# Two attention and gMLP layers on one core: the later weights' scales found by a DMA read-back in two batches, and the weights' splits moved within the first layer

## The chip, the core and the metric

The kernel runs on one core of a Trainium2 chip. The metric is the device time of one execution, in microseconds (us), as the median of several runs. "Layer" below means one attention block followed by one gMLP block; the program runs two layers with the same weights.

## What is computed

With `phi(t) = t + 1` for positive t and `exp(t)` otherwise, and x of 2048 rows by 640 columns:

```
x = A_x
x = x + A(layernorm(x));  x = x + B(layernorm(x))
x = x + A(layernorm(x));  x = x + B(layernorm(x))

A(x):  q, k, v = x @ wq, x @ wk, x @ wv            # 32 heads of 20
       for 4 segments of 512 rows:
           o = (1 - g) * softmax(q k^T * scale + mask) v + g * (phi(q) M) / (phi(q) z)
           M, z += phi(k)^T v, sum phi(k)
       return o @ wo                                # wo 640 x 640
B(x):  z = gelu(x @ w_in)                           # w_in 640 x 1728
       z1, z2 = z[:, :864], layernorm(z[:, 864:])
       return (z1 * (w_sp @ z2 + b_sp)) @ w_out     # w_out 864 x 640
```

Products run in fp16 with each operand held as a high and a low half. A weight is first scaled by a power of two that comes from its largest absolute value, then split: `h = fp16(w * s)` on ScalarE, `l = fp16(w * s - h)` on VectorE (`split_scaled`, L80). So before a weight can be split, its largest element over all 128 partitions must be known on every partition.

## The kernel before

Each layer has three phases: `phase1a` (attention, class `Attention`), `phase1b` (the last rows' output projection, layernorm, both halves of w_in) and `phase2` or, in the second layer, `phase2s` (the w_sp product and w_out).

**The attention** is a software pipeline in steps. `Attention.run` (L1376) walks t from below 0 to past 192. In each step PE multiplies one chunk of a pair of heads: `mp` (scores for the row maxima, read by VectorE's `mx` reduction at L1304) and `es` (scores for the exponentials, read by ScalarE's `P` at L1297). Then come the fp16 halves of P (`PH` on ScalarE at L1314, `PL` on GpSimd at L1315), and the product with v (`pv`, L1341). One `P` activation belongs to one step, so 192 of them make one attention. Tiles `mp`, `es` and `pv` have one buffer each: PE's next chunk waits for the readers of the last one.

Around the pipeline several generators are run, each yielding the step at which it wants to go on: `fills` (next rows' layernorm), `background` (the weights), `dense` (the q, k, v and output projections in between) and `reads`. PE's order is as written; the other engines' instructions are ordered at build time by a list scheduler, which works with priorities (`tc.high_priority`, and `issue_after` for what must not go earlier). Each engine's queue, and SP's queue that issues nearly all DMAs, is then run in order: an instruction that waits holds up all behind it.

**The weights, in the first layer only.** `head` (L950) scales and splits wq, wk and wv before step 0. In `background` (L1459), `other_scales` (L179) loads all of wo, w_in and w_out in 32 tiles from step -8 on, 0.75 step apart, and reduces each on VectorE (`wap<-wmst`, L192) in a pool of two buffers that other tiles use as well. At steps 50 to 53 the maximum is carried over the partitions by TensorE: a transpose (`wtp`), a reduction, a scaled identity (`wdg`), and a product with ones (`wbc`). From step 55 on wo is loaded again and split in five tiles, and from step 69 the half of w_in called i1 in ten (`Weight.load`, L106). The other half, i0, is split by `phase1b` in five tiles of 864 columns after the attention. `keep` (L130) writes the halves to DRAM; the second layer reads them back instead.

**The end of the attention.** `phase1b` first brings the first two tiles of rows to the transposed form `th` (`load`, `attn_out`, `xn_t`): a load of x1, layernorm (`lnst`, `lnmv`, `lnve` on VectorE, `lnrs` on GpSimd, `xn` on VectorE), its halves `xnhl` (ScalarE, VectorE) and a DMA transpose. `first` is a context that lets these begin in the last steps of the attention. Then PE multiplies, for each tile of 128 rows, 30 matmuls with i1 and 30 with i0 (`zp`, L316).

Of the kernel before, what the change touches and what calls it, by code (L numbers as in the profile page):

```python
# [9 lines left out]
F32 = mybir.dt.float32  # L10
# [36 lines left out]
WNAMES = ["v", "q", "k", "o", "i0", "i1", "u"]  # L47
# [18 lines left out]
def pow2_spread(g, psum, tag, dg, c0, n):  # L66
# [3 lines left out]
    nc.tensor.matmul(bc[:, :n], g.ones8[:n, :], dg[:n, :n], start=True, stop=True)  # L70
    pw = g.pw[:, c0:c0 + n]
    nc.vector.tensor_copy(pw, bc[:, :n])
# [15 lines left out]
class Weight:  # L88
# [17 lines left out]
    def load(self, stage, width=864, tag="wst", keep=True):  # L106
# [4 lines left out]
        if self.made:  # L111
# [30 lines left out]
def attn_weights(g, ctx, wv, wq, wk, wo, w_in, w_out):  # L142
# [6 lines left out]
    g.wi = [Weight(g, "i0", 4, w_in, 0, FH), Weight(g, "i1", 5, w_in, FH, FH)]  # L149
# [4 lines left out]
    g.esc, g.rq, g.rk, g.gq, g.gk, g.sig, g.epsd, g.yw, g.zi, g.pofs = s(0), s(1), s(2), s(3), s(4), s(5), s(6), s(7), (s(8), s(9)), s(10)  # L154
# [24 lines left out]
def other_scales(g, a, pool, psum, tag):  # L179

    nc = g.nc
    last = None
    for i, w in enumerate((g.wo, *g.wi, g.wu)):
        width = D if w.cols == D else w.cols // 2
        j = 0
        for k in range(w.nk):
            n = min(128, w.dram.shape[0] - 128 * k)
            for c in range(0, w.cols, width):
                t = a.bg.tile([128, D], F32, tag="bg", name="wmst")[:n, :width]
                nc.sync.dma_start(t, w.dram[k * 128:k * 128 + n, w.c0 + c:w.c0 + c + width])  # L190
                if last is not None:
                    nc.vector.tensor_reduce(*last, AX.X, ALU.max, apply_absolute_value=True)  # L192
                last = g.wap[:n, i, j:j + 1], t
                yield True
                j += 1
    nc.vector.tensor_reduce(*last, AX.X, ALU.max, apply_absolute_value=True)
    yield 50
    nc.vector.tensor_reduce(g.wam[:, 3:7], g.wap, AX.X, ALU.max)
# [4 lines left out]
    nc.vector.tensor_scalar(g.yw, g.pw[:, 0:1], g.pw[:, 3:4], 2.0 ** -19, ALU.mult, ALU.mult)  # L203
    nc.vector.tensor_scalar(g.sc[:, 8:10], g.pw[:, 4:6], 2.0 ** -24, None, ALU.mult)
# [1400 lines left out]
```

## Time and profile before

| | us |
|---|---|
| median of 3 runs | 2323.73 (2322.91 to 2328.16) |
| the profiled execution | 2331.88 |
| its span, first to last instruction | 2330.2 |

Roughly, in us from the span's start: weights and first rows until 112, where step 0's `P` runs; attention until 649; `phase1b` until 855; `phase2` until 1262; the second attention until 1781, its `phase1b` until 1985, `phase2s` to the end. The engines are PE (TensorE matmul), PEld (its weight load), DVE (VectorE), ACT (ScalarE), POOL (GpSimd) and SP (the DMA queue). In a row "L84 ACT ... x10" the first field is the line of the kernel, x10 the count.

### The profile page before, as it was taken

The numbers are of one execution on the slowest core, as the hardware profiler recorded it, in microseconds if no ns is written. First come the engines' busy times: TensorE is split into PE (matmuls) and PEld (weight loads), VectorE is DVE, ScalarE is ACT, GpSimd is POOL, SyncE is SP. The second block draws the span as 40 slices with busy tenths as digits, with TensorE's granted clock in tenths as the row PEclk, the third lists the DMA queues.
The fourth block names the chain that finished last, engine by engine and source line by source line (L and its number), as shares of the span: only waits on it lengthen the run. The fifth ranks groups of instructions, "written<-read, shape, count | busy, mean of one in ns | idle before, by whom it ended". The sixth has DMA issues, their size and how long they took to land.

```text
span 2330.2 us, 50381 instructions
## 1 busy us (share of the span) xinstructions
PE 2173.5 (93%) x20490; PEld 1297.3 (56%) x20490; DVE 1503.4 (65%) x2791; ACT 1174.3 (50%) x1452; POOL 971.5 (42%) x726
## 2 busy tenths in 40 slices
PE   4878899899889999999999989999998999999998
PEld 2445465556645555555655555656665555555655
DVE  8678868877644545454434788787776757555454
ACT  3279778787632232122212797887875324322221
POOL 2178778888710000000001688888895323000000
PEclk9999899999999999999999999999999999999999
DMA  5654544544563457878655336354466434977875
GB/s 162 166 138 102 131 107 128 129 144 117 146 168 90 132 160 196 244 189 243 162 144 157 75 92 181 103 125 95 122 170 166 116 102 102 264 205 188 227 200 124
DMA packets 509561, 350.16 MB, mean 150 GB/s; under 512 B 409296, under 2 KB 444496, under 8 KB 504208
## 3 DMA queue, kind: packets, MB, share of 16 engines
q1 hardware_dynamic: 509328, 346.93, 56.4%
q8 instruction: 161, 2.64, 0.5%
q14 instruction: 72, 0.59, 0.1%
HBM read 160.83 MB, written 97.93 MB: 111 GB/s over the span
## 4 chain that ended last, share of the span: by engine, by line
PE 65%; DVE 11%; DMA 8%; ACT 7%; issue 3%; SPq 1%; POOL 1%; ACTq 0%; DVEq 0%; POOLq 0%
PE zp L316 14%; PE gp L683 10%; PE pv L1341 4%; PE cyp L715 3%; PE yps L1098 3%; PE cyp L519 3%; DVE mx L1304 3%; PE ga L469 3%; PE mp L1288 3%; PE kps L1122 3%; ACT P L1297 2%; PE qps L1122 2%; PE vps L1065 2%; PE gb L469 2%; ACT PH L1314 2%
## 5 line engine op out<-in xcount | busy, mean ns | idle before, releaser
L1315 POOL TENSOR_TENSOR PL<-P,PH 128x1280 f16<-128x1280 f32 x248 | 649.5, 2621 | 167.8 <-ACT PH L1314 154.7
L1304 DVE TENSOR_REDUCE mx<-mp 128x2 f32<-128x1024 f32 (+3 forms) x512 | 408.8, 818 | 97.2 <-PE mp L1260 95.6
L1297 ACT ACTIVATE P<-es,sc 128x1024 f32<-128x1024 f32 (+1 forms) x384 | 370.3, 964 | 135.3 <-PE es L1260 133.2
L1314 ACT CAST PH<-P 128x1280 f16<-128x1280 f32 x256 | 320.4, 1253 | 21.6 <-PE pv L1341 12.9
L219 POOL TENSOR_TENSOR lnrs<-lnve,mhalf 128x1 f32<-128x1 f32 x92 | 56.1, 618 | 576.2 <-DVE lnve L218 576.2
L316 PEld LDWEIGHTS <-th 128*128 128x128 f16 x1920 | 188.5, 98 | 177.2 <-issue 16.4
L683 PE MATMUL gp<-zh,wt 128*128 128x432 f16 x1024 | 231.4, 346 | 0.3 <-DMA wt<-wn 0.3
L683 PEld LDWEIGHTS <-wt 128*128 128x128 f16 x1536 | 150.1, 98 | 129.8 <-DMA wt<-wn 1.1
L1288 PEld LDWEIGHTS <-qk 60*128 60x128 f16 (+1 forms) x2048 | 91.1, 93 | 225.8 <-issue 154.3
L469 PEld LDWEIGHTS <-wt 128*128 128x128 f16 x1344 | 131.5, 98 | 112.6
L1288 PE MATMUL mp<-qk 60*128 60x512 f16 (+3 forms) x1024 | 138.2, 307 | 41.1 <-DVE mx L1304 40.1
L1341 PE MATMUL pv<-vs,PH 128*128 128x41 f16 x2560 | 168.6, 183 | 2.1 <-DVE ab L1357 2.0
L1260 PEld LDWEIGHTS <-big 64*128 64x128 f16 x3072 | 141.5, 96 | 50.9 <-issue 3.9
L1341 PE MATMUL pv<-vs,PL 128*128 128x41 f16 x2560 | 164.4, 182 | 4.4 <-POOL PL L1315 3.9
L1288 PE MATMUL es<-qk 64*128 64x512 f16 (+3 forms) x1024 | 135.7, 300 | 35.0 <-ACT P L1297 25.4
L1065 PE MATMUL vps<-wvh,xt 128*128 128x320 f16 x640 | 151.5, 302 | 3.6 <-DVE vs L1071 3.0
L1341 PEld LDWEIGHTS <-PH 128*128 128x128 f16 x2560 | 142.9, 96 | 18.7
L316 PE MATMUL zp<-wi1h,th 128*128 128x432 f16 x640 | 149.2, 348 | 2.1 <-DVE x L1104 1.3
L1341 PEld LDWEIGHTS <-PL 128*128 128x128 f16 x2560 | 143.4, 97 | 7.8 <-POOL PL L1315 4.7
L683 PE MATMUL gp<-zl,wt 128*128 128x432 f16 x512 | 135.3, 346 | 0.0
L1122 PE MATMUL kps<-xt,wkh 128*128 128x512 f16 x380 | 124.0, 395 | 9.1 <-DVE phl L1156 9.0
L696 DVE TENSOR_TENSOR u<-u,cz 128x864 f32<-128x864 f32 x16 | 17.0, 1060 | 160.8 <-ACT u L694 120.4
(253 smaller groups left out, 4386.2 us busy)
## 6 DMA issues: line engine op xcount, KB each, us to landing
wr<-in_B_w_sp_dram SPq DMA_DIRECT2D x32, 1024.0 KB
qk<-st SPq DMA_DIRECT2D x256, 120.0 KB
x<-x SPq DMA_DIRECT2D x56, 320.0 KB
z<-z SPq DMA_DIRECT2D x32, 432.0 KB
cz<-z SPq DMA_DIRECT2D x32, 432.0 KB
turned<-wt SPq DMA_DIRECT2D x24, 512.0 KB
wt<-turned SPq DMA_DIRECT2D x24, 512.0 KB
st<-qhl SPq DMA_DIRECT2D x40, 256.0 KB
```

What stands on the lines that cost most here:

```text
L316: nc.tensor.matmul(zp[:, n, :FHH], a[:, k, :], b[:, k, c:c + FHH], start=(k == 0 and j == 0), stop=(k == KD - 1 and j == 2))
L469: nc.tensor.matmul(o[:, :FHH], wt[:, x, m, :], zb[b][:, y, m, :], start=start and i == j == 0, stop=i == NP - 1 and j == 2, skip_group_che ...
L683: nc.tensor.matmul(gp[:, n, :FHH], ready[t][:, k % 2, a, k // 2, :], b[:, k, n * FHH:(n + 1) * FHH], start=(i == 0 and j == 0), stop=(i == ...
L1065: nc.tensor.matmul(ps, a[:, k, c], b[:, k, n * 320:(n + 1) * 320], start=(i == 0), stop=(i == 14))
L1122: nc.tensor.matmul(ps, a[:, k, c], b[:, k, :], start=(i == 0), stop=(i == 14))
L1260: nc.tensor.matmul(out, g.big[r, 64 - 64 * s:192 - 64 * s], mk, start=False, stop=s == 1, skip_group_check=True)
L1288: nc.tensor.matmul(out[:, h, o:o + w], a[r, ac], b[r, bc], start=o == 0, stop=False, skip_group_check=True)
L1297: self.last_of["ACT"] = nc.scalar.activation(P[:, :, 512 * c:512 * c + ew], es[:, :, :ew], AF.Exp, scale=g.esc).ins
L1304: self.last_of["DVE"] = nc.vector.tensor_reduce(self.mx[m][:, :, i], mp[:, :, o:o + w], AX.X, ALU.max).ins
L1314: nc.scalar.copy(PH, P[:, h])
L1315: (nc.gpsimd if h == 0 or n < self.N - self.TAIL else nc.vector).tensor_tensor(PL, P[:, h], PH, ALU.subtract)
L1341: nc.tensor.matmul(pv[:, i, h, :], x[:, c:c + 128], v[:, j, h0 + h, :], start=(j == 0 and x is PH), stop=(j == i and x is PL), skip_group_ ...
```

## The change

- `other_scales` takes a list of weights and runs twice: for wo and i1 (15 tiles) from step -8, 1.9 steps apart, and for i0 and w_out (17 tiles) from step 121, 2.2 steps apart. Its tiles have a pool of their own with three buffers, and a tile is reduced two loads after its own.
- The maximum goes over the partitions by DMA: `wam` is written to DRAM (`wmax`), read back to all partitions (`wmall`), and reduced on VectorE. TensorE's transpose and product for this go.
- wo is split from step 50, 1.6 steps apart; i1 from step 124, 2.4 steps apart (both with one tile loaded ahead, from a pool of three buffers). These splits are a stream of their own.
- i0 is split in ten tiles of 432 columns, in the last steps of the attention, behind the `first` context, and after the code of the first two tiles of rows.
- Some pools are put in another order (so tiles lie elsewhere in memory), and the writes of i0 and i1 to DRAM stand later in the code.

```diff
-WNAMES = ["v", "q", "k", "o", "i0", "i1", "u"]
+WNAMES = ["v", "q", "k", "o", "i1", "i0", "u"]
...
-    def load(self, stage, width=864, tag="wst", keep=True):
+    def load(self, stage, width=864, tag="wst", keep=True, ahead=0):
...
+        todo = []
...
                 nc.sync.dma_start(st, self.dram[k * 128:k * 128 + n, self.c0 + c:self.c0 + c + w])
+                todo.append((self.h[:n, k, c:c + w], self.l[:n, k, c:c + w], st, self.c))
                 yield
-                split_scaled(self.g, self.h[:n, k, c:c + w], self.l[:n, k, c:c + w], st, self.c)
-                yield
+                if len(todo) > ahead:
+                    split_scaled(self.g, *todo.pop(0))
+                    yield
+        for x in todo:
+            split_scaled(self.g, *x)
+            yield
...
-def other_scales(g, a, pool, psum, tag):
+def other_scales(g, a, ws, c0, at, pace):
...
-                t = a.bg.tile([128, D], F32, tag="bg", name="wmst")[:n, :width]
+                t = a.wm.tile([128, D], F32, tag="wm", name="wmst")[:n, :width]
                 nc.sync.dma_start(t, w.dram[k * 128:k * 128 + n, w.c0 + c:w.c0 + c + width])
-                if last is not None:
-                    nc.vector.tensor_reduce(*last, AX.X, ALU.max, apply_absolute_value=True)
-                last = g.wap[:n, i, j:j + 1], t
-                yield True
+                last.append((g.wap[:n, i, j:j + 1], t))
+                if len(last) > 2:
+                    nc.vector.tensor_reduce(*last.pop(0), AX.X, ALU.max, apply_absolute_value=True)
+                yield at
+                at += pace
...
-    yield 51
-    dg = pow2_max(g, pool, psum, tag, g.wam, 3, 4)
-    yield 53
-    pow2_spread(g, psum, tag, dg, 3, 4)
+    yield at + 3
+    t = a.wm.tile([128, D], F32, tag="wm", name="wmall")[:, :128 * n]
+    d = nc.dram_tensor(f"wmax{c0}", (128, n), F32, kind="Internal").ap()
+    nc.sync.dma_start(d, g.wam[:, c0:c0 + n])
+    nc.sync.dma_start(t, d.rearrange("(o p) n -> o (p n)", o=1).to_broadcast((128, 128 * n)))
+    yield at + 9
+    nc.vector.tensor_reduce(g.pw[:, c0:c0 + n], t.rearrange("q (p n) -> q n p", n=n), AX.X, ALU.max)
+    pow2_floor(g, c0, n)
...
-            p2, p1, px2, px1, sp = pool("b2", 2), pool("b1", 1), pool("bx2", 2), pool("bx1", 1), pool("bs", 2)
-            pe2, pe1, wp0 = pool("be2", 2), pool("be1", 1), pool("bw0", 1)
+            p2, p1, px2, px1 = pool("b2", 2), pool("b1", 1), pool("bx2", 2), pool("bx1", 1)
+            pool("bp", 1).tile([128, 256], F32, name="bp")
+            pe2, pe1, sp, wp0 = pool("be2", 2), pool("be1", 1), pool("bs", 3), pool("bw0", 1)
...
-        with tc.high_priority(offset=HP if w0 is None else 2 * HP):
-            for _ in g.wi[0].load(sp):
-                pass
...
+        with tc.high_priority(offset=2 * HP) if w0 is not None else first():
+            for _ in g.wi[0].load(sp, FHH, "ws", False, 1):
+                pass
...
+            if w0 is None and i in (3, 6):
+                g.wi[i == 3].keep()
...
-            if not g.wo.made:
+            if first:
                 nc.vector.memset(g.wap, 0.0)
-                for i, _ in enumerate(other_scales(g, self, self.pl1, self.pm, "ms")):
-                    yield -8 + 0.75 * i if _ is True else _
...
-            yield 54
-            for j, (w, width, pace) in enumerate(((g.wo, D, 1.3), (g.wi[1], FHH, 3))):
-                w.tiles(g.top[j])
-                for i, _ in enumerate(w.load(self.bg, width, "bg")):
-                    yield 55 + 14 * j + pace * i
+                yield from other_scales(g, self, (g.wo, g.wi[1]), 3, -8, 1.9)
...
+                yield 120
+                yield from other_scales(g, self, (g.wi[0], g.wu), 5, 121, 2.2)
...
+        def weights():
+
+            g = self.g
+            yield 49
+            for w, width, at, pace in (g.wo, D, 50, 1.6), (g.wi[1], FHH, 124, 2.4):
+                w.tiles(g.top[w is not g.wo])
+                for i, _ in enumerate(w.load(self.ws, width, "ws", w is g.wo, 1)):
+                    yield at + pace * i
```

PE's order is the same but for the two rows of the transpose and the product that go. What follows shows the built order at three places on other engines; the names are those of the lines above, and lines after the change are about 20 higher for the same code.

VectorE near step 50, before. `wam` to `iv` are the exchange of the maximum over the partitions, among the pipeline's own rows:

```order
L198 TENSOR_REDUCE wam<-wap 128x4
L1304 TENSOR_REDUCE mx<-mp 128x2
L1352 TENSOR_TENSOR rs<-pv,iomg 128x8
L1353 RECIPROCAL rs<-rs 128x8
L1357 TENSOR_TENSOR ab<-pv,rs 128x328
L1325 SCALAR_TENSOR_TENSOR mr<-mtp,mr 8x128
L60 TENSOR_REDUCE wmx<-wtp 4x1
L62 TENSOR_SCALAR wdg<-ident,wmx 4x4
L1139 SCALAR_TENSOR_TENSOR qhl<-qps,qhl 128x512
L1144 TENSOR_SCALAR qps<-qps,sc 128x512
```

The same place after:

```order
L1377 TENSOR_TENSOR ab<-pv,rs 128x328
L91 SCALAR_TENSOR_TENSOR wol<-wst,iv,woh 128x640
L1324 TENSOR_REDUCE mx<-mp 128x2 x2
L234 BN_STATS lnst<-xt 128x6 x2
L1345 SCALAR_TENSOR_TENSOR mr<-mtp,mr 8x128
L1159 SCALAR_TENSOR_TENSOR qhl<-qps,qhl 128x512
L1164 TENSOR_SCALAR qps<-qps,sc 128x512
```

The exchange is gone from here (it stands near step 29 and step 167 now, as `pw<-wmall`), and the first of wo's splits has come.

ScalarE at the end of the first attention, before; the two `P` rows are those of steps 190 and 191:

```order
L1314 CAST PH<-P 128x1280
L1297 ACTIVATE P<-es,sc 128x2x512
L231 CAST xnhl<-xn 128x640
L1297 ACTIVATE P<-es,sc 128x2x256
L1314 CAST PH<-P 128x1280 x2
L1368 CAST ohl<-oat 128x640
L84 ACTIVATE wi0h<-wst,iv 128x864 x2
L322 ACT_TABLE_LOAD
```

After:

```order
L1334 CAST PH<-P 128x1280
L90 ACTIVATE wi0h<-wst,iv 128x432 x2
L1317 ACTIVATE P<-es,sc 128x2x512
L90 ACTIVATE wi0h<-wst,iv 128x432
L1317 ACTIVATE P<-es,sc 128x2x256
L1334 CAST PH<-P 128x1280
L90 ACTIVATE wi0h<-wst,iv 128x432
L1334 CAST PH<-P 128x1280
L1388 CAST ohl<-oat 128x640
L249 CAST xnhl<-xn 128x640 x2
L338 ACT_TABLE_LOAD
```

i0's splits have moved from behind the attention in among its last steps, and both `xnhl` of the first rows from among the last steps to behind them.

SP's queue at the end of the first attention, after; `x_11186<-x_0_0` and `x_11199<-x_0_1` are the loads of the first two tiles of rows for `phase1b`:

```order
L130 DMA wst<-in_B_w_in_dram 128x432
L148 DMA w_i0h<-wi0h 128x4320
L148 DMA w_i0l<-wi0l 128x4320
L1126 DMA x_0_10<-x_10911 128x640
L1392 DMA o_3<-ohl 128x4x160 x2
L291 DMA x_11186<-x_0_0 128x640
L291 DMA x_11199<-x_0_1 128x640
L1126 DMA x_0_11<-x_11032 128x640
L297 DMA_TRANSPOSE o<-o_3 128x10x128
L294 DMA xt<-in_A_x_dram 128x640 x2
L291 DMA x_11302<-x_0_2 128x640
L251 DMA_TRANSPOSE th<-xnhl 128x10x128
```

Before, those two loads stood ahead of the attention's last four `qk<-mr` DMAs; now they stand behind its last output (`o_3<-ohl`). The first also waits for VectorE's last row of the attention (`x_11032<-yps`), since its tile now lies where a tile of the attention lay.

More of the change, by code (lines that the diff above doesn't have):

```diff
@@ L334, in phase1b @@
         ts = [*range(NWO - 4), *range(NWO, NT), *range(NWO - 4, NWO)]
-        with first:
+        with first():
             a = load(ts[0])
@@ L1478, in run @@
         g = self.g
+        first = not g.wo.made
+        self.wm, self.ws = [self.pool(n, 3) for n in ("awm", "aws")] if first else [None, None]
         g.top = [self.top.enter_context(g.tc.tile_pool(name=n, bufs=1, side="right", reuse_waits="tile")) for n in ("topi", "topo")][::-1]
-        streams = [[next(it), i, it] for i, it in enumerate((fills(), background(), dense(), reads()))]
+        streams = [[next(it), i, it] for i, it in zip((0, 1, 1.5, 2, 3), (fills(), background(), weights(), dense(), reads()))]
         def until(t):
@@ L1496, in run @@
             if t == 3 * N - 9:
-                self.first, self.end_of = self.ended(), [*self.last_of.values()]
+                self.first, self.end_of = self.ended, [*self.last_of.values()]
             f, c = divmod(t + self.LF, 3)
```

35 lines of the change are left out of this document (20 added, 15 removed).

## Prediction

> **What bounds the kernel now.** I read the page first: is one engine full?
>
> ```profile
> span 2330.2 us, 50381 instructions
> PE 2173.5 (93%) x20490; PEld 1297.3 (56%) x20490; DVE 1503.4 (65%) x2791; ACT 1174.3 (50%) x1452; POOL 971.5 (42%) x726
> ```
>
> PE is busy for 93% of the span, so at most some 157 us of PE's idle time can be won, and PE's own work hardly changes. The question is how much of that idle time the weights' work of the first layer makes. The two attentions run the same pipeline; only the first prepares weights. So the second is the measure. I took the stretches view of the exponentials' line (L1297), with the stretches cut so that both layers have the same count in each (one `P` per step; columns: stretch, length, ACT busy and count, clock, DMA share, GB/s). First layer, steps 0 to 18, 48 to 54, 54 to 72, 72 to 132, 132 to 180 and 180 to the end:
>
> ```profile
> 112.00:163.80 51.80, 17.36 (x18) 0.93 0.61 159
> ...
> 232.40:252.50 20.10, 5.79 (x6) 0.92 0.43 102
> 252.50:320.40 67.90, 17.37 (x18) 0.85 0.59 146
> 320.40:488.20 167.80, 57.82 (x60) 1.00 0.48 124
> 488.20:607.10 118.90, 46.33 (x48) 1.00 0.50 128
> 607.10:640.00 32.90, 11.62 (x12) 0.85 0.52 133
> ```
>
> Second layer, the same steps:
>
> ```profile
> 1292.00:1332.20 40.20, 17.36 (x18) 1.00 0.35 78
> ...
> 1401.00:1415.60 14.60, 5.76 (x6) 1.00 0.57 160
> 1415.60:1469.80 54.20, 17.40 (x18) 0.97 0.65 175
> 1469.80:1632.00 162.20, 57.98 (x60) 1.00 0.43 106
> 1632.00:1750.30 118.30, 46.33 (x48) 1.00 0.55 147
> 1750.30:1781.00 30.70, 11.62 (x12) 0.89 0.58 142
> ```
>
> The first layer is late by 11.6 us in steps 0 to 18, 5.5 in 48 to 54, 13.7 in 54 to 72, 5.6 in 72 to 132, 0.6 and 2.2 after that: 39 us. The losses lie where the weights are worked on, and 132 to 180, where nothing of the weights runs, loses almost nothing. I call this the **lag**; it is what the change can win in the attention. (Steps 18 to 48 lose nothing.)
>
> **Steps -8 to 48: the early maxima.** The tile view of `wmst` (durations min/median/max, first and last start; then, by what ended it, the idle time before these rows and its count), and behind it that of `wst`:
>
> ```profile
> L192 DVE TENSOR_REDUCE wap<-wmst x31: 584/603/821, 71.4 to 160.4; 128x1 f32<-128x432 f32 x20, 128x1 f32<-128x640 f32 x11
> ...
>   DMA wmst<-in_B_w_in_dram: 8.2, 6
>   DMA wmst<-in_B_w_out_dram: 3.3, 3
> ```
>
> ```profile
> L84 ACT ACTIVATE wi1h<-wst,iv x10: 642/652/655, 311.8 to 464.1; 128x432 f16<-128x432 f32 x10
> L85 DVE SCALAR_TENSOR_TENSOR wi1l<-wst,iv,wi1h x10: 652/669/2210, 312.5 to 464.9; 128x432 f16<-128x432 f32 x10
> ...
> L84 ACT ACTIVATE woh<-wst,iv x5: 818/828/830, 261.1 to 298.0; 128x640 f16<-128x640 f32 x5
> L85 DVE SCALAR_TENSOR_TENSOR wol<-wst,iv,woh x5: 875/885/1391, 261.9 to 299.8; 128x640 f16<-128x640 f32 x5
> ```
>
> 32 reductions take 20 x 0.60 + 12 x 0.82 = 21.8 us of DVE, and DVE stood 11.5 us waiting for their loads: 33.3 us of its queue for 11.6 us of lag, **0.35 us per us of DVE**. After: 5 x 0.82 + 10 x 0.60 = 10.1 us, the waits gone, as a tile is read two loads (3.8 steps, some 8 us) after its own. The read-back adds a two-column reduction (not in this trace; I take twice the 0.28 that `wmx`, a row of 128, takes in the groups further below; bounds 0.28 and 0.82) and five small rows of 0.16, some 1.4 us. 11.5 x 0.35 = 4.0. **Gain 7.6**; bounds of what stays 2 to 8.
>
> **Steps 48 to 72.** The exchange over TensorE goes. Four of its rows, and GpSimd's `PL`, from the groups of 240 to 253 us (last columns: busy us, mean ns of one, idle us before):
>
> ```profile
> L1315 POOL TENSOR_TENSOR PL<-P,PH 128x1280 f16<-128x1280 f32 x3 | 7.8, 2610 | 1.2 <-ACT PH L1314 1.2
> L62 DVE TENSOR_SCALAR wdg<-ident,wmx 4x4 f32<-4x4 f32 x1 | 2.4, 2382 | 0.0
> L204 DVE TENSOR_SCALAR sc<-pw 128x2 f32<-128x2 f32 x1 | 2.4, 2356 | 0.0
> ...
> L60 DVE TENSOR_REDUCE wmx<-wtp 4x1 f32<-4x128 f32 x1 | 0.3, 279 | 0.4 <-PE wtp L58 0.4
> ...
> L74 DVE TENSOR_TENSOR pw<-pw,floor 128x4 f32<-128x4 f32 x1 | 0.2, 164 | 0.0
> ```
>
> `wdg` and `sc` take 2.4 us for sixteen and two elements: held up, not computing. With `wmx` (0.28) and seven small rows like the last (0.16 each), the exchange took 6.2 us of DVE, near the 5.5 us of lag in 48 to 54. In 54 to 72, wo's five splits take 4.4 us of DVE and 4.1 of ACT, and one split of i1 waited for its load (the chain of waits, start and length):
>
> ```profile
> 303.56 8.27 DMA wst<-in_B_w_in_dram
> ```
>
> 13.7 = 8.3 + 5.4: the rest is about wo's splits at full price. After: wo's splits stay, two or three steps earlier and loaded ahead; the exchange and i1 are gone. I take 5.5 for what stays (bounds 2 and 4.4 + 4.1 = 8.5). **Gain 19.2 - 5.5 = 13.7.** What is late next there: DVE itself, 82% busy in the second layer's 1401 to 1470.
>
> Here the Trainium skill speaks against the change: SBUF — State Buffer, section "Who interferes with whom", says that VectorE and GpSimd share a pair of ports under an exclusive lock, that `tensor_scalar` can take it, and that the later one waits for the whole instruction; a `PL` on GpSimd takes 2.6 us in the groups above, and the two rows of 2.4 us agree. By that rule each of the read-back's small rows could wait up to 2.4 us, twice per kernel now: with two of them held per batch the sum would be 4 x 2.2 x 0.35 = 3 us worse; by the 0.16 of the other rows nothing.
>
> **Steps 72 to 120.** i1's splits go from here. **Gain 5.6.**
>
> **Steps 121 to 172: what comes.** 17 reductions (10 x 0.60 + 7 x 0.82 = 11.8 us), the second read-back (1.4) and i1's ten splits (6.7 on DVE, 6.5 on ACT). The same steps in the second layer (columns: PE, PEld, DVE, ACT, POOL):
>
> ```profile
> 1602.00:1729.60 127.60, 126.51 (x1815) 79.64 (x1812) 96.92 (x192) 105.11 (x129) 112.30 (x75) 1.00 0.47 131
> ```
>
> PE is full here, DVE 76%, ACT 82%: 30.7 us of room for 19.9 on DVE, 22 for 6.5 on ACT. All loads are two steps or more ahead, so none should wait. Between nothing (hidden by PE) and 19.9 (all of DVE on the path) I take the 0.35 of the early reductions: **loss 7.0**. SP also waits twice for `wmax` to land before it can issue `wmall`; behind it stand `qk<-mr` and `qk<-st` of coming steps. The shortest landings in the chain take 2 to 3 us and `mr` has two steps' time: **loss 1**, bounds 0 and 5.
>
> **The end of the attention.** Before, PE goes from `yps` straight to `zp`, but stands for i0. `zp` in the stretches view, the chain at four places, the groups of 612 to 640 us, and two rows of the timeline:
>
> ```profile
> 649.30:671.50 22.20, 12.70 (x56) 0.98 (x1) 0.85 0.66 196
> 671.50:676.00 4.50, 4.43 (x16) 0.98 (x1) 0.62 1.02 411
> 676.00:690.00 14.00, 14.00 (x78) 1.95 (x2) 1.00 0.64 137
> ```
>
> ```profile
> 637.07 3.23 DMA x<-x
> ...
> 648.80 0.56 DVE x L1104
> ...
> 650.28 6.59 DMA o<-ohl
> ```
>
> ```profile
> 1946.46 3.52 DMA th<-xnhl
> ```
>
> ```profile
> L232 DVE TENSOR_TENSOR xnhl<-xn,xnhl 128x640 f16<-128x640 f32 x2 | 1.8, 898 | 0.0
> L216 DVE BATCH_NORM_STATS2 lnst<-x 128x6 f32<-128x320 f32 x4 | 1.8, 468 | 2.8 <-DMA x<-x 2.8
> ...
> L225 DVE TENSOR_SCALAR xn<-x,lnmv,lnrs 128x640 f32<-128x640 f32 x2 | 1.2, 611 | 0.1
> ```
>
> ```profile
> 631.01 0.72 ACT L231 CAST xnhl<-xn 128x640 f16<-128x640 f32 x1 [0.21 <-DVE xn L225]
> ```
>
> ```profile
> 661.55 1.06 POOL L219 TENSOR_TENSOR lnrs<-lnve,mhalf 128x1 f32<-128x1 f32 x2 [11.63 <-DVE lnve L218]
> ```
>
> After, i0 is ready, but the first rows are not: SP loads `x` only behind the last `o<-ohl`, at 650.7. Landing 3.2 (653.9); three `lnst` 1.4 and two rows on means, an estimate of 0.3 by `pw`'s 0.16; `lnrs` 0.53; `xn` 0.61; `xnhl` 0.72 and 0.90; transpose 3.52: PE starts at 661.9. 56 matmuls at 14.0/78 = 0.18 take 10.0: 671.9, where the kernel before had 56 at 671.5 and then lost another 4.5 - 16 x 0.18 = 1.6 at a clock of 0.62. That alone is -1.2. Two things are added. ACT's ten splits of i0 (0.65 each) stand among the last steps: two ahead of the last pair's `P` (1.3), one whose load waits for the seventh split's buffer and lands about 1.1 late: +2.4 (bounds 0 and all ten, 6.5). The 2.8 us for which DVE waited for `x<-x` goes, but ACT's first split waits for a load issued at that very place: nil. And PE, idle for some 13 us, comes back slow: twice the 1.6, at most 3.2; I take +2. **Loss 3.2**, bounds -1.2 and 12 (with a landing of 4.8). TensorE: Matmul & The Clock Gate, section "What's actually happening", of the Trainium skill gives half speed for about 3.4 us after such a gap, 1.7 us lost as an estimate; the slow stretch 671.5 to 676 comes later than that after PE's restart, so the row asks for more.
>
> **The sum.** -7.6 - 13.7 - 5.6 + 7.0 + 1.0 + 3.2 = -15.7. From the profiled execution's 2331.9 that is 2316.2; the median of the runs is 8.2 lower, so 2323.7 - 15.7 = **2308**. Elsewhere the order is the same; the second layer reads one half of i1 back later, at a step where DMA is half idle: nil.
>
> **Rivals.**
> - **Dear splits (slower).** In steps 121 to 172 each split of i1 costs what six splits cost in 54 to 72, 13.7/6 = 2.3 us, as ACT and DVE wait for a load in order; ten are 23, 17 reductions at 11.6/32 are 6.2, the read-back 0.5: 29.7 instead of 7.0, and the time 2331. It decides when this stretch costs more than 27 us. For it: ACT, DVE and POOL are all three near 80 to 90% there. Against it: the loads come ahead from three buffers, and the 8.3 of the 13.7 was one such wait.
> - **The end eats it (no change).** Landing, ACT's splits and the slow PE at their upper bounds, 12, and SP's waits 5: 2321. For it: all ten splits stand on a chain in which PE waits already.
> - **Hidden.** PE, full in 121 to 172, covers the late work (2 instead of 7), the early part keeps 2: -22.7, 2301. For it: 132 to 180 shows no lag; but it has no such work either.
> - **Not done.** The scheduler could have left the splits where they were; the built order shows that it has not.
>
> **How the numbers follow.** Forecast 0.61, hidden 0.20, the end 0.12, dear splits 0.07. A measurement here tells 0.2% (4.6 us) from no change. Faster by that: forecast and hidden, less a little for the forecast's upper tail, 0.80; within: the end and that tail, 0.13; slower: 0.07. The range leaves out the dear splits and the sum of all lower bounds: 2295 (sum with 2, 2, 0, 0 and -1.2 would be 2290) to 2324.
>
> **What would show it.** The same stretches of `P`: lag of about 4 in steps 0 to 18, 5 to 6 in 48 to 72, 0 in 72 to 120, 7 in 120 to 180. DVE's wait for `wmst` near 0. A gap in PE of 11 to 14 us between the last `yps` and the first `zp`, ended by `th<-xnhl`, and no wait for i0 behind it. Wrong if the lag in 120 to 180 passes 15 or that gap passes 20 us.

## The result and the profile after

| | us |
|---|---|
| before, median of 12 runs | 2325.04 (2320.29 to 2328.59) |
| after, median of 12 runs | 2326.80 (2323.10 to 2329.68) |
| ratio after to before | 1.0007, 95% interval 0.9998 to 1.0015 |
| profiled execution of after | 2323.44, span 2321.4 |

The change moves the time by nothing that can be measured. I had forecast 2308, 2295 to 2324. The page of the changed kernel begins:

```profile
span 2321.4 us, 50393 instructions
...
PE 2167.8 (93%) x20487; PEld 1295.0 (56%) x20487; DVE 1506.8 (65%) x2800; ACT 1175.8 (51%) x1457; POOL 973.0 (42%) x726
```

The stretches view of its exponentials (L1317 now), first layer, cut at steps 0, 18, 48, 54, 72, 120, 156, 180 and 191 (columns: stretch, length, ACT busy and count, clock, DMA share, GB/s):

```profile
108.30:151.20 42.90, 17.36 (x18) 0.96 0.46 111
151.20:227.30 76.10, 28.84 (x31) 0.93 0.34 87
227.30:243.00 15.70, 5.76 (x6) 1.00 0.68 202
243.00:303.30 60.30, 17.43 (x19) 0.92 0.54 141
303.30:435.50 132.20, 46.44 (x48) 0.99 0.45 112
435.50:529.00 93.50, 34.82 (x37) 1.00 0.59 162
529.00:598.20 69.20, 23.18 (x24) 0.95 0.61 155
598.20:627.60 29.40, 10.92 (x12) 0.94 0.66 174
```

One trace against one says -8.4 us here, the medians say +1.8: executions scatter. So I took a second trace of each kernel first (`rep_before`, `rep_after` below). All lengths in us, from the starts of `P` and `zp` in the four traces:

| stretch | before | again | after | again | predicted | measured (second traces) |
|---|---|---|---|---|---|---|
| start to step 0 | 112.1 | 111.9 | 108.3 | 110.9 | | -1.0 |
| steps 0 to 18 | 51.8 | 51.3 | 42.9 | 45.1 | -7.6 with 18 to 48 | -6.2 |
| 18 to 48 | 68.7 | 68.4 | 76.1 | 76.0 | | **+7.6** |
| 48 to 72 | 87.9 | 88.5 | 76.0 | 75.8 | -13.7 | -12.7 |
| 72 to 120 | 136.9 | 137.4 | 132.3 | 132.0 | -5.6 | -5.4 |
| 120 to 156 | 88.6 | 88.8 | 93.5 | 92.8 | +8.0 with 156 to 180 | +4.0 |
| 156 to 180 | 61.3 | 59.7 | 69.2 | 69.3 | | **+9.6** |
| 180 to 191 | 31.5 | 30.2 | 29.4 | 29.1 | | -1.1 |
| last `P` to the 73rd `zp` | 37.5 | 36.0 | 41.2 | 41.1 | +3.2 with 180 to 191 | +5.1 |
| from there to the end | 1654.0 | 1650.9 | 1652.6 | 1650.6 | nil | -0.3 |

The stretches come again within 1.6 us, but for the first two rows of after (2.6 and 2.2) and the last row (3.1 and 2.0); the 7 us by which before's first trace is longer lie in many places (steps 156 on, the transition, the last phase). The gains came as forecast. Two stretches ate them: 18 to 48 and 156 to 180, where the two read-backs stand.

What stops TensorE in steps 18 to 48, in the waits view of after (us in total, times, longest):

```profile
PE mp L1308 <- DVE mx L1324: 5.1, 6, 3.5
PE es L1308 <- DMA qk<-mr: 4.0, 2, 2.8
```

The same two rows in before:

```profile
PE mp L1288 <- DVE mx L1304: 1.5, 4, 0.6
PE es L1288 <- DMA qk<-mr: 1.1, 1, 1.1
```

In steps 156 to 180, the second trace of after has:

```profile
PE es L1308 <- DMA qk<-mr: 3.7, 2, 2.5
PE mtp L1342 <- DVE gm L1217: 2.5, 1, 2.5
```

In these steps of the second trace of before one wait is listed:

```profile
PE mp L1288 <- DVE mx L1304: 0.4, 1, 0.4
```

Each of the stops can be followed back. First SyncE's queue at the first read-back (timeline of after: start, length):

```profile
158.49 0.35 SPq L218 DMA_DIRECT2D wmax<-wam  x1
161.44 0.34 SPq L219 DMA_DIRECT2D wmall<-wmax  x1
161.88 1.12 SPq L1347 DMA_DIRECT2D qk<-mr  x2
```

The queue stands from 158.8 to 161.4, and the two `qk<-mr` stand behind it. At the second read-back the chain of waits of `rep_after` tells the same, with the price of each link:

```profile
542.28 3.02 DMA wmax<-wam
...
545.31 0.33 SPq L219
...
546.37 4.06 DMA qk<-mr
...
550.56 0.61 PE es L1308 x2
```

Then the small rows, beside GpSimd's `PL` (timelines of VectorE and of GpSimd in after; the first GpSimd row holds two `PL` of 2.6):

```profile
182.31 1.34 DVE L80 TENSOR_TENSOR pw<-pw,floor 128x2 f32<-128x2 f32 x1
...
183.77 0.19 DVE L1486 TENSOR_SCALAR sc<-pw 128x1 f32<-128x1 f32 x1
...
183.99 2.23 DVE L83 TENSOR_SCALAR iv<-iv 128x2 f32<-128x2 f32 x1
...
563.94 2.58 DVE L1490 TENSOR_SCALAR sc<-pw 128x2 f32<-128x2 f32 x1
```

```profile
181.02 5.18 POOL L1335 TENSOR_TENSOR PL<-P,PH 128x1280 f16<-128x1280 f32 x2 [1.44 <-ACT PH L1334]
...
563.86 2.64 POOL L1335 TENSOR_TENSOR PL<-P,PH 128x1280 f16<-128x1280 f32 x1 [0.65 <-ACT PH L1334]
```

`iv` ends at 186.22 and the `PL` at 186.20; `sc` at 566.52 and the `PL` at 566.50. Two elements per partition took 2.2 and 2.6 us because the row waited for a whole `PL`. `mx` and `den`, `gm` stand behind it, and TensorE behind those.

A stop costs more than its length. The stretches view of `rep_after` around both stops of the first batch (clock is the figure behind the five engines), TensorE idle 2.98 us until 170.6 and 3.54 us until 192.2:

```profile
171.00:175.00 4.00, 4.00 (x48) 2.11 (x45) 2.60 (x6) 2.72 (x4) 2.57 (x3) 0.65 0.41 113
175.00:179.00 4.00, 3.05 (x50) 1.69 (x48) 3.33 (x6) 2.76 (x3) 1.82 (x2) 1.00 0.35 103
...
193.00:197.00 4.00, 4.00 (x60) 2.35 (x57) 2.29 (x4) 3.66 (x6) 1.74 (x2) 0.50 0.56 124
```

Some 4 us follow at a clock of 0.65 and of 0.50: 4 x 0.35 = 1.4 and 4 x 0.5 = 2.0 us more, an estimate from these rows alone. Together 2.98 + 3.54 + 3.4 = 9.9, of which 7.6 is net, as the kernel before has waits in these steps too.

### The profile page after: what moved, and what is told of

The parts are those of the page before. It is cut to its first block, busy times and chain, and to the rows that moved or that the text cites. A ratio compares the mean times of both kernels' runs of the same rounds, so it can differ in the third digit from the quotient of the medians.

```text
span 2321.4 us, 50393 instructions
## 1 busy us (share of the span) xinstructions
PE 2167.8 (93%) x20487; PEld 1295.0 (56%) x20487; DVE 1506.8 (65%) x2800; ACT 1175.8 (51%) x1457; POOL 973.0 (42%) x726
## 3 DMA queue, kind: packets, MB, share of 16 engines
q8 instruction: 160, 2.62, 0.5%
## 4 chain that ended last, share of the span: by engine, by line
PE 60%; DVE 4%; ACT 4%; DMA 2%; issue 1%; POOL 1%; SPq 0%; ACTq 0%; DVEq 0%; POOLq 0%
PE zp L332 14%; PE gp L704 12%; PE cyp L736 4%; PE cyp L540 4%; PE ga L490 3%; PE gb L490 3%; PE pv L1361 2%; PE vps L1085 2%; PE yps L1118 2%; PE qps L1142 2%; PE kps L1142 2%; PE gd L490 2%; PE gc L490 2%; PE mp L1308 2%; PE yp L309 1%
## 5 line engine op out<-in xcount | busy, mean ns | idle before, releaser
L1317 ACT ACTIVATE P<-es,sc 128x1024 f32<-128x1024 f32 (+1 forms) x384 | 370.8, 966 | 135.7 <-PE es L1280 132.7
L1334 ACT CAST PH<-P 128x1280 f16<-128x1280 f32 x256 | 320.5, 1253 | 20.4 <-PE pv L1361 11.6
L332 PE MATMUL zp<-wi1h,th 128*128 128x432 f16 x640 | 149.4, 348 | 13.7 <-DMA th<-xnhl 13.1
```

The costliest lines, as they stand in the source:

```text
L332: nc.tensor.matmul(zp[:, n, :FHH], a[:, k, :], b[:, k, c:c + FHH], start=(k == 0 and j == 0), stop=(k == KD - 1 and j == 2))
L1317: self.last_of["ACT"] = nc.scalar.activation(P[:, :, 512 * c:512 * c + ew], es[:, :, :ew], AF.Exp, scale=g.esc).ins
L1334: nc.scalar.copy(PH, P[:, h])
```

## The experiments

The lengths below are read as in the table, and compared with the second trace of after. Ratios are to the kernel before.

**Second traces.** No edit.

> The kernel before, unchanged, for a second trace. Its first profiled execution lay 6.8 us above the median of the twelve runs, that of the changed kernel 3.4 below, so the difference of the two traces (-8.8) is not that of the medians (+1.8). Theory scatter: executions differ in a few stretches only; the stretches of P of the second layer come again within 1 us, and the missing 7 us show in the head (112.1 us to the first P), in the first layer's stretches where DMA is busy, or in the last phase. Rival: the first trace was representative in the first layer (within 2 us in every stretch), and the 7 us lie outside the attention.

> The changed kernel, unchanged, for a second trace. Theory: the three stops show again at the same places: TensorE waits about 2.8 and 3.1 us for qk<-mr behind the two read-backs, 3.5 and 2.5 us behind the held small rows of VectorE, and 12.5 us before the first zp. Rival: the stops of 2.5 to 3.5 us are chance of one execution; then they are under 1 us or elsewhere here.

Measured: 2324.80 and 2324.69, spans 2323.1 and 2322.7. The stretches are in the table. Before's extra 7.1 us lie where scatter was expected only in part: 2.6 of them between the last `zp` of the second layer and the end, 4.5 spread over both layers, no stretch of the table's attention over 1.6. After's stops came again at the same instructions, 2.98, 3.54, 2.46 and 2.50 us, and 14.2 before the first `zp`. They are no chance.

**`apart`: the two DMAs of the read-back two steps apart.**

```diff
     nc.sync.dma_start(d, g.wam[:, c0:c0 + n])
+    yield at + 5
     nc.sync.dma_start(t, d.rearrange("(o p) n -> o (p n)", o=1).to_broadcast((128, 128 * n)))
```

> The changed kernel with the load of wmall issued two steps after the write of wmax, in both batches, so that the queue of SyncE has other work between and does not wait for the write to land. Theory SP: the wait of 2.5 and 1.8 us in the queue of SyncE makes the qk<-mr behind it late, and each costs TensorE about 3 us and a slower clock for some us after it: 5 to 8 us less than the changed kernel (about 2320). Rival slack: the qk<-mr are two steps early and the wait is absorbed elsewhere: within 1.5 us of the changed kernel.

Measured: 2320.60, ratio 0.9982 (0.9966 to 0.9997). Steps 18 to 48 take 72.2 us instead of 76.0, and the waits on `qk<-mr` there fall from 4.0 to 1.0:

```profile
PE mp L1309 <- DVE mx L1325: 5.7, 7, 3.5
...
PE es L1309 <- DMA qk<-mr: 1.0, 1, 1.0
```

Steps 156 to 180 did not move (69.6). The theory holds for the first batch; in the second the queue still stands, 1.9 us ahead of the write of `wam`.

**`narrow`: the small rows one column at a time.**

```diff
+    if n > 1:
+        return [pow2_floor(g, c0 + i, 1) for i in range(n)][-1]
     pw = g.pw[:, c0:c0 + n]
...
-                nc.vector.tensor_scalar(g.sc[:, 8:10], g.pw[:, 4:6], 2.0 ** -24, None, ALU.mult)
+                for i in range(2):
+                    nc.vector.tensor_scalar(g.sc[:, 8 + i:9 + i], g.pw[:, 4 + i:5 + i], 2.0 ** -24, None, ALU.mult)
```

> The changed kernel with the small rows behind the read-back (pw, iv and the two zi scales) done one column at a time, 128x1 instead of 128x2: twice as many rows, the same values. Theory held rows: a two-column row that meets a PL on GpSimd ends with it (four of four did), a one-column row does not (sc 128x1 took 0.18 beside a PL); no row of these is over 0.3 us then, TensorE's stops of 3.5 and 2.5 us go, 5 to 8 us less than the changed kernel (about 2320). Rival: the stop comes with the place, not with the row's shape: a one-column row is held as well, 2 us or more, and the time is the same or some 1 us more.

Measured: 2323.38, ratio 0.9995 (0.9980 to 1.0009). Steps 18 to 48 take 72.7, and the wait on `mx` falls from 3.5 to 1.5:

```profile
PE es L1310 <- DMA qk<-mr: 3.6, 2, 2.6
PE mp L1310 <- DVE mx L1326: 3.4, 7, 1.5
```

The tile view of `iv` says why: no one-column `tensor_scalar` is held any more, though some start beside a `PL`.

```profile
L85 DVE TENSOR_SCALAR iv<-iv x7: 96/144/154, 19.8 to 562.8; 128x1 f32<-128x1 f32 x7
```

My "no row over 0.3" was wrong for one row: `pw<-pw,floor`, which reads two tensors, still took 1.29 us with one column, to the end of its `PL`. In steps 156 to 180 the stop behind `gm` went too, but the one before an `es` at 574 us, 1.2 in `rep_after`, grew to 4.0: 71.8 us. There another wait had been hidden behind it. The whole is as before within its interval, not the 5 to 8 us that I expected.

**`apart_narrow`: both.** The two diffs above.

> The changed kernel with both edits, the read-back's load two steps after its write and the small rows one column wide. In the first batch each of the two took 3.5 us out of steps 18 to 48 (76.0 to 72.2 and 72.7), TensorE's stops of 3.0 and 3.5 us going one at a time. Theory: two separate stops, so the gains add there: 68.5 to 69.5 us, as before the change (68.4). In the second batch the narrow rows took their stop away as well (2.5 us), but two others, before es, stood in both runs; there I expect no more than 3 us less than the 69.3 of steps 156 to 180. Rival: both edits removed the same loss and the sum is no better than one, 72 us. Whole: 5 to 9 us under the changed kernel, about 2319.

Measured: 2319.27, ratio 0.9974 (0.9961 to 0.9987). Steps 18 to 48: 69.8 (68.4 before the change). The gains add; the first batch is settled. Steps 156 to 180: 69.3, nothing.

**`pe_exchange`: TensorE's exchange at the places of the read-back.** The body of the read-back becomes

```diff
+    dg = pow2_max(g, a.pl1, a.pm, "ms", g.wam, c0, n)
+    yield at + 5
+    pow2_spread(g, a.pm, "ms", dg, c0, n)
```

> The changed kernel with the exchange of the maxima over the partitions done by TensorE as before (transpose, row reduction, scaled identity, product with ones), at the two places where the read-back stands. Theory: the read-back costs 7.6 us in steps 18 to 48 and up to 9.6 in 156 to 180. TensorE's exchange has no wait in the queue of SyncE, but it has more small rows that a PL can hold (wdg, pw, iv, sc), and TensorE itself waits for them: 73 to 75 us and 66 to 70 us in these stretches, so 2 to 6 us under the changed kernel. Rival: its stops are as long as the read-back's, 76 and 69, no gain; or it costs nothing, 68.5 and 60.

Measured: 2323.86, ratio 0.9998 (0.9987 to 1.0008). Steps 18 to 48 take 72.5 and 156 to 180 take 67.3, 3.5 and 2.0 less than in `rep_after`: at these places the read-back is dearer than the exchange that it replaced, by little, and neither is free. The whole is as before's within the interval.

**`local`: no exchange at all** (`narrow`, and each partition takes its own maximum, so the scales are others than the reference's).

> The changed kernel with narrow rows and no exchange over the partitions at all: each partition takes its own maximum for the scale (a copy of wam), so the write, the read-back and the reduction of 256 elements are left out, and the scales are not those of the reference. Theory: what is left of the loss then is not the exchange: steps 18 to 48 come back to 68.4 to 69; steps 156 to 180 keep what the 2.2 MB of writes of i1 (issued by SyncE at 564 us, the qk<-mr of two steps behind them) and the last splits cost: 62 to 66 instead of 69.3 (59.7 before the change). Rival: steps 156 to 180 come down to 60 as well, and the read-back is the whole loss.

Measured: 2318.64, ratio 0.9963 (0.9947 to 0.9979). Steps 18 to 48: 69.7. Steps 156 to 180: 67.9, with one stop of 3.9 us for a `qk<-mr`. So there is a loss in the second batch that is not the exchange: SyncE issues `w_i1h` and `w_i1l`, 2.2 MB, ahead of that `qk<-mr`, with only two `o<-ohl` between (SyncE's queue in `local`):

```profile
560.28 0.35 SPq L150 DMA_DIRECT2D w_i1h<-wi1h  x1
560.72 0.38 SPq L150 DMA_DIRECT2D w_i1l<-wi1l  x1
561.15 2.47 SPq L1390 DMA_DIRECT2D o<-ohl  x2
563.67 2.53 SPq L1345 DMA_DIRECT2D qk<-mr  x2
```

Their code stands in `phase1b`; the scheduler took them forward.

**`late_keep`: these writes held in their place.**

```diff
             if w0 is None and i in (3, 6):
-                g.wi[i == 3].keep()
+                with tc.issue_after(out):
+                    g.wi[i == 3].keep()
```

(`out` is the store of that round's `z1`.)

> The changed kernel with the writes of i1 and i0 to DRAM (2.2 MB each) issued where the code of phase1b has them, behind the fourth and the seventh z1 store, and not, as the scheduler placed them, among steps 170 and 188 of the attention. In all runs with a second read-back TensorE stands before an es at about 572 to 579 us (1.2 us in the changed kernel, 4.1 with the other two stops taken away), for a qk<-mr that is issued right behind these writes. Theory: the writes make that qk<-mr late; in steps 156 to 180 it is 1 to 3 us less than 69.3 here, as the two other stops stay, and nothing comes back in phase1b, where DMA has room: 1 to 4 us under the changed kernel. Rival: the qk<-mr is late from VectorE's and ScalarE's queues; the stop stays, the time is the same.

Measured: 2329.67, ratio 1.0020 (1.0010 to 1.0030). The stop before that `es` is gone, but the two ahead of it stay, and the stretch is 68.7 (69.3 in `rep_after`); `phase1b` takes 1.9 us more. By itself it loses, where I expected 1 to 4 us. With the other two stops gone, that stretch gains by it (`local_late` below); what it is worth to the whole is not shown, as `local_late` ran only once.

**`early`: the first rows of `phase1b` in memory that is free earlier.**

```diff
-            pool("bp", 1).tile([128, 256], F32, name="bp")
-            pe2, pe1, sp, wp0 = pool("be2", 2), pool("be1", 1), pool("bs", 3), pool("bw0", 1)
+            pool("bp", 1).tile([128, 336], F32, name="bp")
+            pt, pe2, pe1, sp, wp0 = pool("bt", 2), pool("be2", 2), pool("be1", 1), pool("bs", 3), pool("bw0", 1)
...
-            th = pe2.tile([128, 2, KD, 128], F16, tag="th", name="th")
+            th = (pt if w0 is None else pe2).tile([128, 2, KD, 128], F16, tag="th", name="th")
```

> The changed kernel with phase1b's pools laid so that the first tiles of rows don't lie where the attention's last rows lie: x1, xn, xnhl and th of the first tile come into memory that is free some steps earlier, and the scheduler puts their loads, layernorm and transpose among the last steps. Theory: in the changed kernel the start of zp waits 12.5 us only for this chain; with it gone zp starts some 0.7 us behind the last yps, i0 is there already, and no stop for i0 follows: from the last P to the 72nd zp some 24 us instead of 41.1, so 13 to 17 us under the changed kernel, about 2311. Rival: in the last steps ScalarE and VectorE have no room for these rows beside i0's splits, the attention ends later by as much, or i0 comes late: less than 5 us under.

In after, the chain of waits ahead of the first `zp` is the one that the prediction laid out, but for its start: the load of the first rows is let go by VectorE's last `x` of the attention, whose memory it takes, and not by the store of `o` as the prediction had it.

```profile
641.48 0.56 DVE x L1124
...
642.45 3.85 DMA x<-x
...
650.26 3.59 DMA th<-xnhl
...
653.89 1.26 PE zp L332 x3
```

Measured: 2332.74, ratio 1.0034 (1.0021 to 1.0048). The wait before `zp` fell from 12.5 (14.2 in the second trace) to 3.2, and the last `P` to the 73rd `zp` took 29.7 instead of 41.1. But `phase2` gave back 21.1 us, most of it in four waits right after `phase1b` (the second row below):

```profile
PE zp L332 <- DMA th<-xnhl: 3.2, 1, 3.2
```

```profile
PE gp L704 <- DMA wt<-wn: 16.6, 4, 8.0
```

i0 lies 320 bytes higher there, over the first tile of the normalized w_sp (`wn`), which so waits for the last `zp`; `early2` tries this.

**`early2`: as `early`, i0 at its old address** (its staging tiles 432 columns wide, and a filler behind them).

```diff
-                st = stage.tile([128, 864 if tag == "wst" else D], F32, tag=tag, name="wst")[:n, :w]
+                st = stage.tile([128, {"wst": 864, "wsb": width}.get(tag, D)], F32, tag=tag, name="wst")[:n, :w]
...
+            pool("bq", 1).tile([128, 544], F32, name="bq")
```

> The kernel of early, with i0's two halves left at their old address. In early the start of the first zp came as forecast (10 us less by the 72nd zp), and 21 us were lost at the start of phase2 in two stops of TensorE before gp (7.1 and 8.0 us): i0 lay 320 bytes higher there, over the first tile of the normalized w_sp, which so had to wait for the last zp. Here i0's staging tiles are 432 instead of 640 columns wide, and i0 stays where it was. Theory: the two stops go and the 10 to 14 us of the start stay: 10 to 14 under the changed kernel, about 2313. Rival: the stops come from the other tiles that moved (x1 and th), and phase2 stays 10 to 21 us longer.

Measured: 2315.24, ratio 0.9954 (0.9941 to 0.9966). `phase2` is back at 436.7, and 11.3 us of the start stay (29.8 instead of 41.1). The theory holds.

**`best`: all of it.** `apart`, `narrow`, `late_keep` and `early2`.

> All edits together: the read-back's load two steps after its write, small rows one column wide, i1's and i0's writes late, and the early first rows of early2. Theory: the gains lie in different stretches and add: 7 in steps 18 to 48, 3 to 6 in 156 to 180 (with the writes gone from there the narrow rows' gain shows), 10 to 14 at the start of phase1b: 20 to 27 us under the changed kernel, 2299 to 2306. Rival: a stop taken away uncovers the next: under 15 us.

Measured: 2304.42, ratio 0.9903 (0.9890 to 0.9917), against both kernels the fastest: the gains add. By the medians the four edits alone lie 6.2, 3.4, -2.9 and 11.6 us under after, 18.3 in sum; together 22.4. Steps 18 to 48: 69.8; 156 to 180: 66.4; last `P` to the 73rd `zp`: 27.2. Still 6.7 us are left in 156 to 180 against before.

**`best2`: the second write of `wmax` two steps later** (its load too, and its reduction one step).

```diff
-    yield at + 3
+    yield at + (3 if c0 == 3 else 5)
...
-    yield at + 5
+    yield at + (5 if c0 == 3 else 7)
...
-    yield at + 9
+    yield at + (9 if c0 == 3 else 10)
```

> The kernel best with the second batch's write of wmax two steps later, so that SyncE does not stand 1.9 us for VectorE's wam before it (its load stays two steps behind it). Theory: that wait made the qk<-mr behind it late, TensorE's stop of 2.3 us at 538.7 us goes and the clock with it: steps 156 to 180 take 62 to 64 us instead of 66.4, about 2301. Rival: the stop comes from the loads and stores that stand ahead of that qk<-mr anyway (x<-x, xt, 0.3 MB each, landing 5.1 us): 66 to 67, no change.

Measured: 2305.17, ratio 0.9918 (0.9903 to 0.9933). The stop of 2.3 us is gone and the stretch takes 62.7; the whole is as `best` within the intervals. In the two traces the 3.7 us won there meet 4.4 us more in steps 54 to 72, which this edit does not touch (60.4 instead of 56.0); what the edit is worth to the whole is not shown.

**`local_late`: `local` with late writes** (so again scales that are not the reference's).

> The kernel local (narrow rows, each partition its own maximum, so other scales than the reference's) with the writes of i1 and i0 late as in late_keep: of the late work it keeps only the 17 reductions, i1's ten splits and the small rows. Theory: nothing of the exchange or the writes is left in steps 156 to 180, and they come to 60 to 62 us as before the change (59.7), against 67.9 with the writes there. Rival: i1's last splits cost some 4 us there too: 64 or more.

Measured: one run, 2320.49. Steps 156 to 180: 60.8, against 59.7 before the change. TensorE's longest waits there:

```profile
PE mp L1307 <- DVE mx L1323: 0.9, 3, 0.4
PE pv L1360 <- DVE ab L1376: 0.6, 1, 0.6
```

So the read-back with its small rows and the writes are 8.5 of the 9.6 us, and reductions and splits 1.1. This holds for the stretch: the whole is no faster than `local`, as the last `P` to the 73rd `zp` took 45.0 us in this execution and the rest 1658.2 (41.1 and 1650.6 in `rep_after`), which was not followed up.

**`noreduce2`: 13 of the 17 late reductions left out** (the scales of i0 and w_out then come from four tiles).

```diff
-                last.append((g.wap[:n, i, j:j + 1], t))
+                if c0 == 3 or j < 2:
+                    last.append((g.wap[:n, i, j:j + 1], t))
```

> The changed kernel without 13 of the 17 reductions of the second batch (the loads stay; the scales of i0 and w_out then come from four tiles alone). Steps 120 to 156 take 92.8 us in the changed kernel and 88.6 before. Theory: 17 reductions and i1's splits of 10 us on VectorE in front of a full TensorE cost these 4 us, most of it the reductions, as they hold the row maxima mx: 89 to 90.5 here. Rival: the splits, which VectorE holds beside a PL (1.6 us instead of 0.67), make it: 92 or more.

Measured: one run, 2330.13. Steps 120 to 156: 96.8 us, no less than 92.8. No saving shows, so the theory falls; but this stretch took from 92.7 to 96.9 us in kernels that do not differ there (`rep_after`, `early2`), so the run alone can't tell a small cost from none. `i1_early` below can. TensorE stops at the same four places with and without them, 1.0, 1.2, 0.9 and 1.1 to 2.8 us, and the first and the third stand right behind splits that VectorE held (1.4 and 1.6 us in `rep_after`, 1.5 and 1.8 here).

**`i1_early`: i1's splits from step 74.**

```diff
-            for w, width, at, pace in (g.wo, D, 50, 1.6), (g.wi[1], FHH, 124, 2.4):
+            for w, width, at, pace in (g.wo, D, 50, 1.6), (g.wi[1], FHH, 74, 2.4):
```

> The changed kernel with i1's ten splits from step 74 on, 2.4 steps apart, instead of from 124 on. Theory: the splits cost the same wherever they stand, as VectorE holds each beside a PL for 0.3 to 1.1 us more and the row maxima wait; steps 72 to 120 rise from 132 to 135 or 137 us and steps 120 to 156 fall from 92.8 to 89 or 90: the sum is within 2 us of the changed kernel's, and the move as such won nothing. Rival: TensorE is fuller late in the attention, so the splits are dearer there than at 74: the sum falls by 3 us or more.

Measured: 2325.73, ratio 1.0001 (0.9990 to 1.0012). Steps 120 to 156 fall to 89.1, near the 88.8 of before: the 17 reductions still stand there, so the 4 us are the splits, in one trace. But steps 72 to 120 take 145.6 us, 13.6 more: there the splits, and the writes of i1, which then stand there too, cost three times what the splits cost from 124 on; before the change, with other steps between them, it was 5.4. TensorE's listed waits there come to 14.9 us instead of 6.2, and one of them, 1.9, is for a `qk<-mr` behind the writes. My "same wherever they stand" fails. The medians do not show the difference of the traces (2325.73, and 2326.80 for after); what the move of the splits by itself is worth stays open.

## Why the prediction failed, point by point

The second traces lie 0.4 us apart, where -15.7 was forecast. Of the 15.3 us between, 8.0 belong to steps -8 to 48 and 5.6 to steps 120 to 180; the other terms came within 1.0 each.

- **Steps -8 to 48, -7.6**: the early maxima gave 7.2 us by step 18 (1.0 before step 0, 6.2 after it). Right; what was lost again behind step 18 is the next point.
- **The read-back's rows, 1.4 us on VectorE at 0.35, and SP's waits, "loss 1, bounds 0 and 5"**: this is the step that failed. Priced at some 2 us for both batches, the exchange cost 7.6 in steps 18 to 48, where `apart_narrow` and `local` take off 6.2 and 6.3, and with the writes of i1 8.5 in 156 to 180. Three things were wrong in it. First, I had said of SP "behind it stand `qk<-mr`" and then let two steps of slack hide it; the slack was not there: at the second read-back TensorE was ready for its `qk<-mr` 1.7 us after the issue, and it took 4.1 to land. Second, the held rows: the prediction quoted two of 2.4 us, read them rightly as held by a `PL`, and priced them by an average, 0.35 us per us of VectorE. A row that stands ahead of `mx` is not an average: TensorE's stops behind these rows were 3.5 and 2.5 us, and 1.5 and none with one-column rows. Third, no stop was charged the slow clock that can follow it, 1.4 and 2.0 us after the first batch's two, though the clock was priced at the end of the attention.
- The Trainium skill's rule that I weighed (SBUF — State Buffer, section "Who interferes with whom") was the right one: VectorE and GpSimd share a port pair, and who comes second waits for the other's whole instruction. In after the three two-column `tensor_scalar` rows that were held beside a `PL` ended with it within 0.03 us, in `narrow` the one-column ones were free, and the `tensor_tensor` on two SBUF tensors was held at either width, as the same section has it. I let it count 3 us as an aside, and left the sum to the 0.16.
- **Steps 48 to 72, -13.7**: -12.7. Right, with 5.5 kept for wo's splits. **Steps 72 to 120, -5.6**: -5.4. Right.
- **Steps 121 to 172, +7.0 for 17 reductions and ten splits**: they cost about 4 in 120 to 156 and 1 in 156 to 180, so 5; near in size, wrong in parts: by `i1_early` the 4 are the splits, and the reductions come to next to nothing.
- **What I had not seen**: the writes of i1 come forward into the attention. The order showed them; I asked of the DMAs that the change moves, but not of those that a scheduler may move. In `narrow` TensorE stops for 4.0 us behind them.
- **The end, +3.2**: last `P` to the 73rd `zp` +5.1, steps 180 to 191 -1.1, so +4.0. The gap is the one forecast (12.5, "11 to 14"; 14.2 in the second trace), ended by `th<-xnhl`, with no wait for i0 behind it; the 56 matmuls after it took 12.0 instead of 10.0, the +2 taken for the slow clock. What starts the chain was named wrongly (the store of `o` instead of VectorE's last `x`), which moved it by little. The upper bound of 12 does not follow from its parts: -1.2, 6.5, 3.2 and 1.6 for the landing make 10.1.
- **The rivals**: "dear splits" had one of the two places, but not the cause; "the end eats it" came nearest in time (2321, that is 2.7 us under the median it starts from; measured 1.8 over), with SP's waits at their bound of 5, and had the wrong place.
- **The signs named beforehand**: neither was passed. The lag of steps 120 to 180 against the second layer is 14.1 and 14.7 us in the two traces of after (15 was the sign), the gap 12.5 and 14.2 (20). No sign was set for steps 18 to 48, where the first loss lies.

## What to carry to other kernels

Price a small instruction on a pipeline's engine by what stands behind it, not by its share of the engine: with one row of two elements held for one GpSimd instruction, TensorE stopped for 3.5 us and lost 2 more to the clock; with one-column rows the stop was 1.5. A queue that issues a write and then the load of it stands until the write lands, with all that is behind; put other work between them. And when stops go one at a time, the next one in line may show (1.2 us became 4.0), so judge such edits together: `apart`, `narrow`, `late_keep` and `early2` gave -0.2, -0.1, +0.2 and -0.5% alone, and -1.0% together, against the kernel before (after itself: +0.1%).

## What the runs showed of the hardware

The hold is a matter of tenths of a us. One split of wo stands in the same order in after and in `late_keep`. In after it starts 0.22 us behind the start of a `PL`, and takes 3.08 us; in `late_keep` it starts 0.17 us ahead of it, and takes 0.87, and the `PL` waits instead (3.17 instead of 2.62). Timeline rows, VectorE and GpSimd of after, then of `late_keep`:

```profile
270.61 3.08 DVE L91 SCALAR_TENSOR_TENSOR wol<-wst,iv,woh 128x640 f16<-128x640 f32 x1
```

```profile
270.39 2.62 POOL L1335 TENSOR_TENSOR PL<-P,PH 128x1280 f16<-128x1280 f32 x1 [0.79 <-ACT PH L1334]
```

```profile
274.97 0.87 DVE L91 SCALAR_TENSOR_TENSOR wol<-wst,iv,woh 128x640 f16<-128x640 f32 x1
```

```profile
275.14 3.17 POOL L1336 TENSOR_TENSOR PL<-P,PH 128x1280 f16<-128x1280 f32 x1 [1.18 <-ACT PH L1335]
```

TensorE's stop behind it is 3.5 us in the one and 1.6 in the other, and steps 54 to 72 take 60.3 and 56.2 us. Of the fifteen traces of the changed kernel and its variants, four have this split free, 0.87 us (`late_keep`, `best`, `apart_narrow`, `i1_early`): steps 54 to 72 take 56.0 to 58.5 us in them, and 59.7 to 63.0 in the other eleven. In `apart_narrow` and `i1_early` the six steps ahead of these took 2.5 to 2.8 us more than in `rep_after`, so only in the other two does it show as a gain of 4 us. That chance of this kind makes the 8 us by which the twelve runs of before differ is possible, and was not tried.

The clock falls sooner than I had thought: behind a stop of 2.98 us it was 0.65 over 4 us, behind one of 3.54 us 0.50. The length of the stop alone does not decide it: in `rep_after` one of 2.46 us was followed by 0.50, one of 2.50 us by 1.00:

```profile
550.50:554.50 4.00, 3.94 (x37) 1.96 (x39) 0.87 (x3) 3.08 (x5) 1.36 (x3) 0.50 0.28 96
571.80:575.80 4.00, 3.97 (x46) 2.60 (x47) 3.72 (x8) 1.38 (x2) 2.06 (x2) 1.00 1.04 363
```

The Trainium skill (TensorE: Matmul & The Clock Gate, section "What's actually happening") gives half rate behind an idle window of about 3.4 us, and about as long until it is full again; of the first batch's two stops, the second agrees, and the first is shorter than that and was followed by a slow clock as well.
